# Front of a two-part kernel: x's maxima in four even pieces, the S4 parameters on GpSimd, and the attention masks loaded ahead of its first operands

## The chip, the cores and the metric

The kernel runs on one core of one Trainium2 chip. The metric is the device time of one launch in microseconds (us); lower is better. Engines are named as the profile names them: PE is TensorE (PEld its weight loads), DVE is VectorE, ACT is ScalarE, POOL is GpSimd, SP is SyncE, which here only issues DMAs. A line such as L743 is a line of the kernel before.

## The reference, cut to what matters

Two independent results stand side by side in the output.

```python
# A: sliding-window attention, x [2048, 576], 32 heads of 18, window 256
qkv = x @ wqkv                                # 576 -> 3 x 576
scores = q k^T * 18**-0.5, masked to 0 <= i-j < 256
a = (softmax(scores) v) @ wo
# B: S4 convolution, u [2048, 576], 128 states per channel
dt = exp(log_dt); dB = dt * B                 # per channel and state
K[d, l] = Re sum_n C * exp(dt*A*l) * dB       # 576 x 2048 filter taps
y = irfft(rfft(u) * rfft(K)) + u * Dskip      # causal convolution
out = concat([a, y], axis=-1)
```

Both are computed in float32 accuracy. For A, x and wqkv are scaled by a power of two, taken from their largest absolute value, and split into two float16 parts (high and low); three float16 products then stand for one float32 product. For B, the exponentials of a filter are built as products of small tables, summed over the states on PE, and the convolution is done by a two-stage transform.

## The kernel before

The program has three stages.

**The front** (`front`, about the first 62 us) loads wqkv in four column pieces (`wf`, in tile K), four row tiles of x (`raw`), the remaining rows of x as one flat array (`flat`, only for their maximum), the small parameters of B, and the S4 rates A. It finds the largest absolute values on DVE (`amax`, L170, into `amx`), reduces them over partitions on POOL (`pow2_max`, L155), and makes the scales: `sw` for wqkv (tile wr of the scalar steps), `sx` for x (tiles xg, xp, xr), `qsc` from both. Meanwhile PE runs `exact` (L217): the first six of the nine query/key products of the first 512 rows, in float32, 30 steps held in six PSUM banks until `qsc` is known; ACT runs the first exponentials (`exps`: tables mab and mg, L434), whose arguments PE makes (L417) from `al`, three bfloat16 parts of dt times A, written back by DMA (`level`). Each piece of wqkv is split by ACT (wh, L199) and DVE (wl, L201). The front is written in a manual order: on each engine the instructions stand as the code names them, except that work of the next stage may be moved up by the scheduler.

At its end the front splits the four row tiles of x (xh on ACT L228, xl and a second xh on DVE L229 and L230), takes exp of dt on ACT (L338) and forms eight products of 128x576 on DVE (L341 to L349): dt times B, and its complex product with C, giving the tiles wr and wi of 128x576 that the factors of B need.

**The middle** (about 62 to 396 us) merges three streams: `proj` (the split projections, L180, which write queries and keys through `qst` to DRAM), `tables` (factors on POOL L465 to L476, products m on POOL L487, tables Q on DVE L507 to L510, taps on PE L525 into `kp`), and `s1_u` (the first transform stage of u, L568). Here the scheduler sets the order on each engine. Held banks are released by `heads`, whose DVE half is `qst` (L367); the first value projections (L180) need such a bank.

**Attention and convolution** (from about 394 us). `att_setup` clears the operand tiles of three attention units; `attention_start` loads unit 0 from DRAM (`load_unit`, L722 and L723); `att_consts` (L701 to L708) clears `bias`, loads its two mask strips and the identity. `gmax` finds each row's largest score: DVE copies Q into qb (L734), PE makes scores r (L743), and DVE adds `bias` and reduces (jk, m, L750). `s1_k`, the transform of the taps K (L568 into pp), is merged with it, after DVE has added the skip term (L1089). The ring of scores has three banks, so PE can run only a few scores ahead of jk. From item 10 on the convolution is merged in (`conv_pools`, `conv`), whose first operands SP loads from L1118 and L595 on.

Each engine runs its instructions in order. [...]

Of the kernel before, what the change touches and what calls it, by code (L numbers as in the profile page):

```python
# [11 lines left out]
F32 = mybir.dt.float32  # L12
F16 = mybir.dt.float16
BF = mybir.dt.bfloat16
I32 = mybir.dt.int32
# [101 lines left out]
class Kernel:  # L117
# [115 lines left out]
    def front(self):  # L233


        nc, a, wp, sp, s4, tp = self.nc, self.a, self.p["wq"], self.p["const"], self.p["s4c"], self.p["prep"]
# [21 lines left out]
        cols = (0, 2304, 4608, 5760, 6912)  # L258
        for c in range(4):
            flat.append(tp.tile([128, 2304], F32, name="flat%d" % (c % 2))[:, :cols[c + 1] - cols[c]])  # L260
            nc.sync.dma_start(flat[c], a["xf"][:, cols[c]:cols[c + 1]])
# [39 lines left out]
        exact = self.exact(raw)  # L301
        for _ in range(15):
            next(exact)
        for c in range(4):
            self.amax(amx[:, c:c + 1], wf[c])
            if c < 3:
                level(c)
            if c < 2:
                for e in (2 * c, 2 * c + 1):
                    self.amax(amx[:, 4 + e:5 + e], raw[:, e])  # L310
        wm, wg = self.pow2_max(amx[:, 0:4], "w")
        pw, self.sw = self.pow2_of(wg, "w")
        steps = chain.from_iterable(zip(exps, exact))
        for _ in range(4):
            next(steps), next(steps)
        self.split_w(2, 0)
        self.amax(amx[:, 8:9], flat[0])
        self.split_w(2, 1)
        for _ in range(4):
            next(steps), next(steps)  # L320
        self.split_w(3, 0)
        self.amax(amx[:, 9:10], flat[1])
        for _ in range(4):
            next(steps), next(steps)
        for _ in chain(steps, exact):
            pass
        self.split_w(3, 1)
        for c in range(2, 4):
            self.amax(amx[:, 8 + c:9 + c], flat[c])
        xm, xg = self.pow2_max(amx[:, 4:12], "x")  # L330
# [9 lines left out]
        wi = self.wi = s4.tile([128, D], F32, name="wi")  # L340
        tt(par["B_re"], par["B_re"], dt, op=OP.mult)  # L341
# [345 lines left out]
    def att_setup(self):  # L687
        nc, a, ap = self.nc, self.a, self.p["att"]
        self.qb = ap.tile([128, 2, 32, 64], F16, name="qb")
        nc.gpsimd.memset(self.qb, 0.0)  # L690
        self.sets = []
        for b in range(3):
# [3 lines left out]
            for h in (32, 96):  # L696
                eng.memset(d["K"][h:h + 32].bitcast(I32), 0xF800F800 - (1 << 32))
# [3 lines left out]
    def att_consts(self):  # L701
# [5 lines left out]
        self.ident = ap.tile([128, 128], F32, name="ident")  # L707
        nc.sync.dma_start(self.ident, a["c_id"])  # L708
# [348 lines left out]
    def build(self):  # L1057
        nc, a = self.nc, self.a
        with ExitStack() as es:
# [36 lines left out]
            with self.tc.manual_schedule():  # L1096
# [3 lines left out]
                self.att_consts()  # L1100
# [12 lines left out]
                def conv_pools():  # L1113
# [4 lines left out]
                    nc.sync.dma_start(self.i2, a["c_i2"])  # L1118

# [38 lines left out]
```

## Time and profile before

| what | us |
|---|---|
| median of three timed runs (lowest, highest) | 979.88 (977.96, 983.45) |
| the profiled execution | 987.38 |
| its span, first to last instruction | 985.7 |
| PE busy in the span | 844.3 (86%) |
| DVE, ACT, POOL busy | 662.9, 566.0, 568.6 |

The profiled execution is 7.5 us above the median, at a mean granted PE clock of 0.965. PE is the busiest engine, but not in each stage: in slices of a fortieth of the span (24.6 us) its busy tenths begin 3758 and drop once more, to 5, just after 400 us. The questions are what PE waits for in the first 100 us, and what it waits for between 396 and 416 us.

### The profile page before, as it was taken

The numbers are of one execution on the slowest core, as the hardware profiler recorded it, in microseconds if no ns is written. First come the engines' busy times: TensorE is split into PE (matmuls) and PEld (weight loads), VectorE is DVE, ScalarE is ACT, GpSimd is POOL, SyncE is SP. The second block draws the span as 40 slices with busy tenths as digits, with TensorE's granted clock in tenths as the row PEclk, the third lists the DMA queues.
The fourth block names the chain that finished last, engine by engine and source line by source line (L and its number), as shares of the span: only waits on it lengthen the run. The fifth ranks groups of instructions, "written<-read, shape, count | busy, mean of one in ns | idle before, by whom it ended". The sixth has DMA issues, their size and how long they took to land.

```text
span 985.7 us, 26852 instructions
## 1 busy us (share of the span) xinstructions
PE 844.3 (86%) x10340; PEld 448.5 (46%) x10340; DVE 662.9 (67%) x1786; ACT 566.0 (57%) x917; POOL 568.6 (58%) x674
## 2 busy tenths in 40 slices
PE   3758897998999999589888888788888899999987
PEld 1235454564566557344433333333333444444445
DVE  5689678367565566456586878788777766667534
ACT  1556767565775765135665565565556555665770
POOL 3018878366677677502367775767675856635460
PEclk9879999899999999798999999999999999999999
DMA  9646354334443532443485665866655674387673
GB/s 314 174 142 177 101 139 115 96 90 113 127 106 78 134 94 77 155 163 124 149 167 144 168 164 145 196 140 171 141 146 138 155 192 106 106 225 199 197 202 129
DMA packets 137177, 145.32 MB, mean 147 GB/s; under 512 B 36553, under 2 KB 105337, under 8 KB 136665
## 3 DMA queue, kind: packets, MB, share of 16 engines
q1 hardware_dynamic: 131000, 131.45, 50.9%
q0 software_dynamic: 4592, 10.32, 3.9%
q10 hardware_dynamic: 1456, 1.84, 0.7%
q8 instruction: 81, 1.33, 0.6%
q14 instruction: 48, 0.39, 0.1%
HBM read 81.29 MB, written 61.01 MB: 144 GB/s over the span
## 4 chain that ended last, share of the span: by engine, by line
PE 45%; DVE 21%; issue 11%; ACT 8%; DMA 7%; POOL 5%; SPq 2%; DVEq 0%; ACTq 0%; POOLq 0%
PE pp L180 8%; PE po L807 6%; PE r L743 6%; PE r L1017 5%; PE kp L525 4%; PE r L609 3%; PE pp L568 3%; PE ST L784 3%; PE r L617 3%; DVE jk L750 3%; PE r L568 2%; PE x L417 2%; ACT P L786 2%; DVE qb L734 2%; DVE osb L866 2%
## 5 line engine op out<-in xcount | busy, mean ns | idle before, releaser
L750 DVE CUSTOM_DVE_ANT_0 jk<-r,bias 128x288 f32<-128x288 f32 (+7 forms) x512 | 199.8, 433 | 98.6 <-PE r L743 89.0
L795 POOL TENSOR_SCALAR_AFFINE_SELECT P<-P 128x512 f32<-128x512 f32 x240 | 166.4, 722 | 165.6 <-ACT P L786 163.2
L786 ACT ACTIVATE P<-ST,esc 128x1024 f32<-128x1024 f32 (+1 forms) x192 | 202.0, 1059 | 83.2 <-PE ST L784 82.9
L487 POOL TENSOR_TENSOR m<-A,tr 128x1024 f32<-128x1024 f32 x72 | 143.7, 2020 | 62.1 <-PE kp L525 62.1
L743 PE MATMUL r<-K,qb 128*64 128x288 f16 (+7 forms) x1024 | 130.9, 298 | 41.6 <-DVE qb L734 12.2
L743 PEld LDWEIGHTS <-qb 128*64 128x64 f16 x1024 | 58.2, 109 | 127.8 <-issue 74.4
L807 PE MATMUL po<-P,V 128*32 128x256 f32 (+2 forms) x1408 | 100.4, 397 | 12.7 <-ACT osb L815 4.4
L646 POOL TENSOR_TENSOR Y<-t,t 64x288 f32<-64x288 f32 x64 | 54.5, 852 | 67.6 <-DVE t L641 65.7
L525 PE MATMUL kp<-Q,m 128*32 128x64 f32 x4608 | 79.4, 221 | 9.5 <-issue 3.1
L525 PEld LDWEIGHTS kp<-Q,m 128*32 128x32 f32 x4608 | 68.8, 110 | 33.1 <-issue 21.4
L784 PE MATMUL ST<-Q,K 64*128 64x384 f16 (+2 forms) x704 | 73.2, 280 | 1.2 <-DMA Q<-mt 1.2
L465 POOL TENSOR_TENSOR tr<-tr,mab 128x768 f32<-128x768 f32 x18 | 33.4, 1858 | 44.0 <-ACT tr L434 44.0
L807 PEld LDWEIGHTS po<-P,V 128*32 128x32 f32 x1408 | 35.7, 109 | 47.1 <-issue 28.3
L647 POOL TENSOR_TENSOR Y<-t,t 64x288 f32<-64x288 f32 x64 | 52.4, 818 | 3.8
L428 DVE TENSOR_TENSOR k<-x,k 128x512 f32<-128x512 f32 (+1 forms) x54 | 33.9, 641 | 23.3 <-ACT k L427 22.8
L568 PE MATMUL pp<-ut,w 128*128 128x288 f32 x128 | 38.8, 429 | 10.6 <-DVE qst L367 6.1
L609 PE MATMUL r<-tx,w 128*64 128x288 f32 x256 | 42.0, 439 | 6.0 <-DVE m L750 3.8
L617 PE MATMUL r<-Y,i 128*128 128x288 f32 x128 | 42.8, 448 | 3.9 <-DVE t L642 1.2
L145 ACT ACTIVATE g<-pp 128x288 f32<-128x288 f32 x69 | 26.7, 412 | 32.5 <-PE pp L568 31.2
L609 PE MATMUL r<-tk,w 128*64 128x288 f32 x256 | 40.8, 424 | 4.8 <-DVE m L750 4.7
L434 ACT ACTIVATE mg<-x 128x512 f32<-128x512 f32 x72 | 39.9, 600 | 7.2 <-PE x L417 6.8
L367 DVE SCALAR_TENSOR_TENSOR qst<-pp,qst 128x512 f16<-128x512 f32 x30 | 20.6, 686 | 34.8 <-ACT qst L366 31.0
(192 smaller groups left out, 1713.8 us busy)
## 6 DMA issues: line engine op xcount, KB each, us to landing
qd<-qst SPq DMA_DIRECT2D x72, 128.0 KB
gx<-g SPq DMA_DIRECT2D x32, 288.0 KB
gk<-g SPq DMA_DIRECT2D x32, 288.0 KB
tx<-gx SPq DMA_DIRECT2D x32, 288.0 KB
tk<-gk SPq DMA_DIRECT2D x32, 288.0 KB
h<-ho SPq DMA_DIRECT2D x16, 576.0 KB
Q<-qd SPq DMA_DIRECT2D x32, 216.0 KB
raw<-in_x_dram SPq DMA_DIRECT2D x16, 320.0 KB
```

What stands on the lines that cost most here:

```text
L180: self.nc.tensor.matmul(ps, u, v, start=(i == 0), stop=(i == len(ops) - 1))
L487: self.nc.gpsimd.tensor_tensor(m, A[:, ch, a0:a0 + 8].unsqueeze(3).to_broadcast(sh), tr[:, ch, part, 0:8].unsqueeze(2).to_broadcast(sh), o ...
L525: nc.tensor.matmul(kp[32 * st:32 * st + 32, c % 2 * JJ2 + j, :], m[:, ch, a0:a0 + 32], Q[:, ch, term % 2, :], start=(term == 0), stop=(ter ...
L568: nc.tensor.matmul(ps, self.w1[:, part, :], src[:, o:o + k], start=True, stop=True)
L609: nc.tensor.matmul(ps[64 * par:64 * par + 64], w2[:, par, 64 * part:64 * part + 64], t[:, par, 2 * hs:2 * hs + 2, :], start=True, stop=True)
L617: nc.tensor.matmul(pair[par], i1[:, par, :], Y[par], start=True, stop=True)
L743: nc.tensor.matmul(ps[64 * b:64 * b + 64, :n], self.qb[:, b, t, :], d["K"][:, b, k0:k0 + n], start=True, stop=True, skip_group_check=True)
L750: nc.vector.tensor_tensor_reduce(out=jk[:, :n], in0=ps[:, :n], in1=self.bias[:, 288 - n:], scale=1.0, scalar=-3e38, op0=OP.add, op1=OP.max ...
L784: nc.tensor.matmul(ps[:, u, o:o + n], d["K"][h, jp, k0:k0 + 128], d["Q"][h, jp, q0:q0 + n], start=True, stop=True, skip_group_check=True)
L786: nc.scalar.activation(pt[:, 2 * jp:2 * jp + 2, lo:hi], ps[:, :, lo:hi], AF.Exp, scale=self.esc)
L795: nc.gpsimd.affine_select(v, v, pattern=[[0, 4], [sg, 128]], compare_op=OP.is_ge, fill=0.0, base=-1 if far else 0, channel_multiplier=-sg)
L807: nc.tensor.matmul(self.po[32 * j:32 * j + 32, t0 * 128:t1 * 128], V[:, kb * 76 + 19 * j:kb * 76 + 19 * j + 32], pt[:, j, o:o + (t1 - t0) ...
```

## The change

Six edits, all of them in placement and order, and a seventh move that follows from one of them; the arithmetic is the same.

1. `flat` has four equal pieces of 1728 columns in three buffers, before two of 2304 and two of 1152 in two buffers.
2. Of `exact`, 18 of 30 steps stand ahead of the first `exps` matmul, before 15; then one step follows every second `exps` matmul, and the rest comes last.
3. The maxima of all four `raw` tiles stand behind the first weight maximum. Both splits of the last two weight pieces start on ACT at once, and the flat maxima stand between their DVE halves.
4. The eight parameter products are POOL's.
5. `att_consts` is called at the start of `att_setup`, ahead of unit 0's loads; the identity is loaded with the convolution's constants.
6. The K tiles of the attention are cleared whole, by one instruction in place of two for 32 partitions each.
7. With 5, the scheduler places the addition of the skip term ahead of the first qb copy.

```diff
-        cols = (0, 2304, 4608, 5760, 6912)
+        cols = (0, 1728, 3456, 5184, 6912)
         for c in range(4):
-            flat.append(tp.tile([128, 2304], F32, name="flat%d" % (c % 2))[:, :cols[c + 1] - cols[c]])
+            flat.append(tp.tile([128, 1728], F32, name="flat%d" % (c % 3)))
             nc.sync.dma_start(flat[c], a["xf"][:, cols[c]:cols[c + 1]])
...
-        for _ in range(15):
+        for _ in range(18):
             next(exact)
         for c in range(4):
             self.amax(amx[:, c:c + 1], wf[c])
             if c < 3:
                 level(c)
-            if c < 2:
-                for e in (2 * c, 2 * c + 1):
+            if c == 0:
+                for e in range(4):
                     self.amax(amx[:, 4 + e:5 + e], raw[:, e])
         wm, wg = self.pow2_max(amx[:, 0:4], "w")
         pw, self.sw = self.pow2_of(wg, "w")
-        steps = chain.from_iterable(zip(exps, exact))
-        for _ in range(4):
-            next(steps), next(steps)
         self.split_w(2, 0)
+        self.split_w(3, 0)
         self.amax(amx[:, 8:9], flat[0])
         self.split_w(2, 1)
-        for _ in range(4):
-            next(steps), next(steps)
-        self.split_w(3, 0)
         self.amax(amx[:, 9:10], flat[1])
-        for _ in range(4):
-            next(steps), next(steps)
-        for _ in chain(steps, exact):
-            pass
         self.split_w(3, 1)
         for c in range(2, 4):
             self.amax(amx[:, 8 + c:9 + c], flat[c])
+        for n, _ in enumerate(exps):
+            if n % 2:
+                next(exact)
+        for _ in exact:
+            pass
         xm, xg = self.pow2_max(amx[:, 4:12], "x")
...
+        tt = nc.gpsimd.tensor_tensor
         tt(par["B_re"], par["B_re"], dt, op=OP.mult)
...
     def att_setup(self):
         nc, a, ap = self.nc, self.a, self.p["att"]
+        self.att_consts()
...
-            for h in (32, 96):
-                eng.memset(d["K"][h:h + 32].bitcast(I32), 0xF800F800 - (1 << 32))
+            eng.memset(d["K"].bitcast(I32), 0xF800F800 - (1 << 32))
...
-        self.ident = ap.tile([128, 128], F32, name="ident")
-        nc.sync.dma_start(self.ident, a["c_id"])
...
                 next(gm)
-                self.att_consts()
...
                     nc.sync.dma_start(self.i2, a["c_i2"])
+                    self.ident = self.p["fc"].tile([128, 128], F32, name="ident")
+                    nc.sync.dma_start(self.ident, a["c_id"])
```

How the change moves instructions is shown at three places. The first is DVE in the front, from the last step of the weights' scale (`wr 128x1`, L166) to the scale of x; `flat_...` are the pieces of x's rest, K is the weights' tile, 128x5x384 and 128x5x576 are the low halves of a weight piece.

```order
 L166 TENSOR_SCALAR wr<-wr 128x1
 L170 TENSOR_REDUCE amx<-flat_139 128x1
-L201 SCALAR_TENSOR_TENSOR wl<-K,wr,wh 128x5x384 x3
+L201 SCALAR_TENSOR_TENSOR wl<-K,wr,wh 128x5x384
 L170 TENSOR_REDUCE amx<-flat_141 128x1
 L201 SCALAR_TENSOR_TENSOR wl<-K,wr,wh 128x5x576
 L170 TENSOR_REDUCE amx<-flat_143 128x1
 L170 TENSOR_REDUCE amx<-flat_145 128x1
+L201 SCALAR_TENSOR_TENSOR wl<-K,wr,wh 128x5x384
 L154 TENSOR_REDUCE xm<-amx 128x1
+L201 SCALAR_TENSOR_TENSOR wl<-K,wr,wh 128x5x384
 L162 TENSOR_SCALAR xg<-xg 128x1
```

Two of the three low halves of 384 columns, which belong to the middle stage, now stand behind the flat maxima: one ahead of the maximum over them (xm), one between xm and the first step that reads POOL's reduction of it (xg).

The second place is DVE after the splits of the row tiles (L229, L230): the parameter products and the first two `qst`, which release held banks.

```order
 L230 SCALAR_TENSOR_TENSOR xh<-raw,xr,xh 64x128
-L341 TENSOR_TENSOR in_B_re<-in_B_re,dt 128x576
-L342 TENSOR_TENSOR in_B_im<-in_B_im,dt 128x576
-L344 TENSOR_TENSOR flat_143<-in_C_re,in_B_re 128x576
-L345 TENSOR_TENSOR flat_145<-in_C_im,in_B_im 128x576
-L367 SCALAR_TENSOR_TENSOR qst<-pp,qsc,qst 128x512
-L346 TENSOR_TENSOR wr<-flat_143,flat_145 128x576
-L347 TENSOR_TENSOR in_C_re<-in_C_re,in_B_im 128x576
-L348 TENSOR_TENSOR in_C_im<-in_C_im,in_B_re 128x576
-L367 SCALAR_TENSOR_TENSOR qst<-pp,qsc,qst 128x512
-L349 TENSOR_TENSOR wi<-in_C_re,in_C_im 128x576
```

The eight TENSOR_TENSOR rows are gone from here. On POOL they now stand behind the reduction xg and an instruction without operands (ISA), and ahead of four small DMA issues (dsk) and the first factor product (`tr<-tr,mab`).

The third place is DVE at the start of the attention, behind the last table of B. Before:

```order
L510 SCALAR_TENSOR_TENSOR Q<-sn,mg 128x16x32
L695 MEMSET Q_5864 128x1024
L697 MEMSET K_5865 32x1280 x2
L734 COPY qb<-Q_5864 54x64x32
L1089 TENSOR_TENSOR K<-K,dsk 128x144
L147 COPY g_5826<-pp 128x288
L734 COPY qb<-Q_5864 54x64x32
L704 MEMSET bias 128x288
```

and with the change (L693 stands for L695, L694 for L697, L1084 for L1089, L729 for L734, L701 for L704):

```order
L507 SCALAR_TENSOR_TENSOR Q<-sn,mg 128x16x32
L701 MEMSET bias 128x288
L693 MEMSET Q_5868 128x1024
L694 MEMSET K_5869 128x1280
L1084 TENSOR_TENSOR K<-K,dsk 128x144
L729 COPY qb<-Q_5868 54x64x32
L147 COPY g_5826<-pp 128x288
L729 COPY qb<-Q_5868 54x64x32
```

The clearing of bias is first, and the addition of the skip term (K<-K,dsk) has passed the first qb copy. On SP the two mask loads stand ahead of unit 0's four loads; before, they stood behind these and behind four stores of `gk`.

## The prediction

> **What bounds the kernel now.** I read the stages first (busy time by window), then the timelines of the engines in the two stages that the change touches, then the chain of waits there. Columns of the windows: length, busy time of PE, PEld, DVE, ACT, POOL (instructions), granted PE clock, DMA share, GB/s.
>
> ```profile
> 20.00:40.00 20.00, 15.46 (x34) 5.70 (x33) 14.37 (x15) 6.47 (x9) 4.29 (x9) 0.83 1.00 287
> 40.00:60.00 20.00, 13.73 (x37) 5.42 (x36) 16.65 (x19) 14.45 (x18) 2.30 (x5) 0.99 0.31 103
> 60.00:80.00 20.00, 14.89 (x91) 10.54 (x91) 16.98 (x31) 12.75 (x25) 7.00 (x8) 0.75 0.59 138
> 300.00:400.00 100.00, 91.65 (x2123) 60.51 (x2111) 64.27 (x98) 62.43 (x111) 76.27 (x57) 1.00 0.39 99
> 400.00:420.00 20.00, 12.71 (x49) 8.42 (x50) 6.38 (x27) 4.12 (x11) 8.22 (x11) 0.70 0.47 155
> ```
>
> The middle is PE's: 91.65 of 100 us. There an earlier start carries through, since behind about 110 us each engine's order is the same as before, up to the attention. The two ends are not PE's: from 20 to 40 us the DMAs are full, from 40 to 80 us DVE is busiest, from 400 to 420 us nobody is. PE's gaps there:
>
> ```profile
> 64.99 1.36 PE L180 MATMUL pp<-wh,xh 128*128 128x288 f16 x5 [9.83 <-DVE qst L367]
> ...
> 400.86 5.84 PE L568 MATMUL pp<-K,w 128*128 128x288 f32 x16 [4.91 <-DVE K L1089]
> ...
> 415.43 0.51 PE L743 MATMUL r<-K,qb 128*64 128x128 f16 x4 [6.23 <-DVE m L750]
> ...
> 417.67 4.11 PE L568 MATMUL pp<-K,w 128*128 128x288 f32 x8
> ...
> 424.46 2.21 PE L568 MATMUL pp<-K,w 128*128 128x288 f32 x8
> ```
>
> The first waits for the first qst, hence for x's scale; the second for the skip term; the third for jk. The same eight matmuls take 4.11 us after the third gap and 2.21 later: a gap also costs 1.90 of slow matmuls.
>
> **Part 1, x's scale (edits 1 to 3).** DVE between the two scales:
>
> ```profile
> 30.24 2.54 DVE L170 TENSOR_REDUCE amx<-flat 128x1 f32<-128x2304 f32 x1
> 37.09 2.22 DVE L201 SCALAR_TENSOR_TENSOR wl<-K,wr,wh 128x1920 f16<-128x1920 f32 x1 [4.30 <-ACT wh L199]
> 41.55 4.38 DVE L201 SCALAR_TENSOR_TENSOR wl<-K,wr,wh 128x1920 f16<-128x1920 f32 x2 [2.25 <-ACT wh L199]
> 45.85 2.55 DVE L170 TENSOR_REDUCE amx<-flat 128x1 f32<-128x2304 f32 x1
> 48.92 3.22 DVE L201 SCALAR_TENSOR_TENSOR wl<-K,wr,wh 128x2880 f16<-128x2880 f32 x1 [0.53 <-ACT wh L199]
> 52.06 2.60 DVE L170 TENSOR_REDUCE amx<-flat 128x1 f32<-128x1152 f32 x2
> 55.34 0.15 DVE L162 TENSOR_SCALAR xg<-xg 128x1 f32<-128x1 f32 x1 [0.48 <-POOL xg L155]
> ```
>
> The columns summed are the same, so DVE's work is: what can go is idle time, 4.30 + 2.25 + 0.53 = 7.1 us of waits for wh, and 0.48 for POOL's reduction, which a low half now covers. ACT made its first wh late because it stood behind an exponential:
>
> ```profile
> 34.78 0.49 ACT L434 ACTIVATE mab<-x 128x384 f32<-128x384 f32 x1 [8.16 <-DMA al<-part]
> 35.17 1.89 ACT L199 ACTIVATE wh<-K,wr 128x1920 f16<-128x1920 f32 x1
> ```
>
> Now two wh stand ahead of it; at 1.89 each and, for the wide one, half as much again (2.8), they end at 30.3 + 4.7 = 35.0, before the exponentials' data is there; DVE wants them at 32.2 (after one flat maximum of 1728 columns, 1.9) and 36. The other two follow by 41, and DVE wants them at 43. The fourth flat piece is the thin spot. Before, its issue waited for the second maximum (45.85 + 2.55 = 48.40):
>
> ```profile
> 48.42 0.35 SPq L261 DMA_DIRECT2D flat<-in_xf_dram  x1
> ```
>
> Now it waits for the first maximum, at 32. From 20 us on the DMAs still have the last weight piece (1.47 MB), flat (3.54), a row tile and parts of al and ps (about 1.0): 6.0 MB at 287 GB/s are 21 us, so it lands near 41, just when DVE gets to it. Price: **-7.6 us** for x's scale; bounds -4.6 (landing 3 us late) and -7.6 (no idle left). The reordered float32 products (edit 2) cost nothing: eight exponentials follow ACT's 41, at 0.65 each (0.49 for 384 columns in the row above, here 512), so the last ends near 46; seven steps of 0.9 (3.60 us for eight halves in the row below) end near 52.5, 2 us before PE can go on.
>
> ```profile
> 51.02 3.60 PE L217 MATMUL kp<-raw,K 128*128 128x512 f32 x8
> ```
>
> **Part 2, the parameters (edit 4).** On DVE the eight products stood between
>
> ```profile
> 61.51 0.76 DVE L341 TENSOR_TENSOR in_B_re<-in_B_re,dt 128x576 f32<-128x576 f32 x1
> ...
> 64.19 0.74 DVE L367 SCALAR_TENSOR_TENSOR qst<-pp,qsc,qst 128x512 f16<-128x512 f32 x1
> ```
>
> so the first qst comes 64.19 - 61.51 = 2.7 us earlier and, with all eight at a pitch of 0.67, what follows 5.4. With part 1 PE's values begin at 64.99 - 10.3 = 54.7, and DVE is 13.0 us ahead. But the factors need wr and wi, and POOL now has a queue ahead of them:
>
> ```profile
> 13.25 1.03 POOL L155 PARTITION_ALL_REDUCE zg<-zm  x1 [9.86 <-DVE amx L170]
> ...
> 55.47 1.95 POOL L355 DMA_DIRECT2D dsk<-in_dsk_dram  x4 [0.17 <-POOL xg L155]
> 72.75 1.82 POOL L465 TENSOR_TENSOR tr<-tr,mab 128x768 f32<-128x768 f32 x1 [15.32 <-ACT tr L434]
> 74.64 0.96 POOL L471 TENSOR_TENSOR t<-tr,wr 128x256 f32<-128x256 f32 x1
> 75.56 0.68 POOL L472 TENSOR_TENSOR t<-tr,wi 128x256 f32<-128x256 f32 x1
> ...
> 77.85 7.87 POOL L487 TENSOR_TENSOR m<-A,tr 128x1024 f32<-128x1024 f32 x4
> ...
> 94.20 1.82 POOL L465 TENSOR_TENSOR tr<-tr,mab 128x768 f32<-128x768 f32 x1 [3.11 <-ACT tr L434]
> ```
>
> One product of 128x576 is not in the trace. Between 0.68 (256 columns) and 1.82 (768) it lies at 1.4; bounds are 1.1 (7.87/4 x 576/1024) and 2.15 (0.96 x 576/256). I take 1.4, the nearest sizes: 11.2 us for eight. An ISA row without operands stands ahead of POOL's first reduction and of its first product, a change of code as I read it. Ahead of the first reduction POOL idled 9.86 us though zm was ready:
>
> ```profile
> 0.97 0.15 DVE L154 TENSOR_REDUCE zm<-halfpi 128x1 f32<-128x1 f32 x1
> ```
>
> Ahead of tr it lay within the 15.32 us idle. Now it comes behind the reduction of x's maximum, at about 46.0 (55.30 - 7.1 - 2.2, xm having one low half less ahead of it), so products can start between 46.0 + 9.9 = 55.9 and dt's exponential, whose end moves from 59.66 to 52.1:
>
> ```profile
> 58.99 0.67 ACT L338 ACTIVATE dt<-dt 128x576 f32<-128x576 f32 x1
> ```
>
> I take the middle, 54.0: the change of code should be shorter than all of that idle time. Then tr starts at 54.0 + 11.2 + 2.0 (dsk's issues) = 67.2, 5.5 earlier. The 3.11 us that POOL waited before the third tr (for DVE) close as well, since DVE is 13.0 ahead: -8.6. PE needs POOL's m for its taps, so POOL, not DVE, sets this stage: **-8.6 us**; bounds: 52.1 + 8.8 + 2.0 = 62.9, that is -9.9 - 3.1 = -13.0; and 55.9 + 17.2 + 2.0 = 75.1, that is +2.4 - 3.1 = -0.7. Part 1 is within this figure, not beside it.
>
> [...] The trace's 9.86 is only an upper limit.
>
> **Part 3, the masks (edits 5 to 7).** DVE and the chain of waits around 400 us:
>
> ```profile
> 399.03 1.56 DVE L734 COPY qb<-Q 54x2048 f16<-54x2048 f16 x1 [1.40 <-DMA Q<-qd]
> 400.52 0.28 DVE L1089 TENSOR_TENSOR K<-K,dsk 128x144 f32<-128x144 f32 x1
> ...
> 415.18 0.19 DVE L750 CUSTOM_DVE_ANT_0 jk<-r,bias 128x32 f32<-128x32 f32 x1 [7.90 <-DMA bias<-in_c_bias_dram]
> ```
>
> ```profile
> 396.22 1.04 ACT L533 ACTIVATE K<-kp 128x512 f32<-128x512 f32 x1 [3.84 <-PE kp L525]
> ```
>
> ```profile
> 408.19 6.82 DMA bias<-in_c_bias_dram
> ```
>
> The skip term needs only ACT's copy, done at 397.26, but stood behind a qb copy that waited for Q. Passed ahead, it ends at 397.6 and PE starts at 397.7: -3.2 of the 4.91. The mask loads now go ahead of unit 0's loads and land while Q does: the 6.23 us go too, and with them the slow matmuls behind that gap, 4.11 - 2.21 = 1.9. Sum **-11.3 us**; bounds -3.2 (another landing replaces the masks') and -12.7 (the sixteen matmuls at 400.86, 5.84 for 2 x 2.21, also run 1.4 faster). The Q and K loads are issued up to 1.0 later (two mask issues at 0.5, as the identity's below), hidden behind PE's sixteen matmuls, which end at 403.5, when qb's second half is done too; without that cover it costs 1.0. Clearing K whole is one instruction per tile, not two, of the same columns: no cost on DVE, some us saved on POOL off the path.
>
> The identity's load now stands on the chain ahead of the first convolution operands:
>
> ```profile
> 408.70 0.50 SPq L708 DMA_DIRECT2D ident<-in_c_id_dram  x1
> ```
>
> **+0.5 us**, bounds 0 and 1.
>
> **Sum**: -8.6 - 11.3 + 0.5 = -19.4 us on a profiled execution of 987.38, that is 968.0. That execution is 7.5 above the median; I take the same difference off 979.88: **960.5 us**. Least -0.7 - 3.2 + 1 = -2.9, 977; most -25.7, 954.
>
> **Rivals.**
>
> *POOL late* (15%): products at 2.15 after the longest change of code. Part 2 gives 0.7, the rest 10.8: 968.4. For it: two 256-column products took 0.96 and 0.68, so contention with DVE can show; against: larger ones stand near 1.9 ns per column. DVE's splits suffer from POOL too:
>
> ```profile
> 56.96 0.75 DVE L229 SCALAR_TENSOR_TENSOR xl<-raw,xr,xh 128x512 f16<-128x512 f32 x1 [0.51 <-ACT xh L228]
> ...
> 83.78 2.49 DVE L229 SCALAR_TENSOR_TENSOR xl<-raw,xr,xh 128x512 f16<-128x512 f32 x1
> ```
>
> 0.75 alone, 2.49 beside POOL's products; the new products bring that ahead of the first qst if POOL starts early (four such instructions, 1.4 each at most: 5.6 us, part 2 then -7.4, since DVE's 13.0 falls to that). [...]
>
> *Masks replaced* (12%): K's or Q's landing holds qb or r instead; part 3 gives 3.2 to 5: 967. For it: the four loads now stand behind the masks, and Q's landing held qb for 1.40 us before; against: PE has 5.8 us of matmuls meanwhile.
>
> *No carry-through* (9%): both gains vanish downstream, or the scheduler's new order up to about 110 us costs what the front saves and masks gain least: 977. Against it: PE's order is equal behind that.
>
> *Slower* (3%): POOL's queue ahead of the factors becomes the bound. It takes over 4.9 us net, so part 2 at +15.7: tr at 72.75 + 3.1 + 15.7 = 91.6, (91.6 - 55.9 - 2.0)/8 = 4.2 us per product. Beyond that: 985. No row is near.
>
> **How the numbers follow.** The forecast (parts 2 and 3 within some 4 us of their values) has 61%, with its own range 955 to 966. A change under 0.5% (4.9 us) can't be told from none here. Faster: 61 + 15 + 12 = 88%; same 9%; slower 3%. The range of 954 to 973 takes in the first two rivals and leaves the others out.
>
> **What would show it.** After the change: x's scale (xr) near 48.3 and no DVE wait over 1 us for wh before it; PE's first L180 near 55; the first tr on POOL at 63 to 70, right behind dsk; no wait of jk for bias; PE's first L568 on K 1.7 us behind the last taps. The prediction is wrong if tr starts after 72, if a wait for Q, K or bias over 3 us stands around 400, or if PE's shift at 390 us is under 5.

## The result and the profile after

The changed kernel takes 976.3 us (median of eight runs, 970.64 to 977.29) beside 983.4 us for the kernel before (median of eight, 977.96 to 984.97): ratio 0.9925, 95% interval 0.9898 to 0.9953, that is 7.1 us less. The forecast was 960.5 with a range of 954 to 973: the direction was right, the size was not, and the time lies 3 us outside the range. Timed once more on another chip (below), the changed kernel was 1.7 us faster by the medians, ratio 0.9969 (0.9936 to 1.0002), an interval that includes no gain. The first trace of the kernel before, from which the forecast was made, is of an execution at 987.4 us that was slow as a whole; two later traces of the same kernel are of 984.0 and 973.4 us, and the two of the changed kernel of 973.6 and 977.4.

Windows of the kernel after, with the columns of the prediction:

```profile
20.00:40.00 20.00, 17.97 (x45) 6.67 (x44) 18.59 (x16) 13.25 (x15) 4.27 (x9) 0.91 1.03 339
40.00:60.00 20.00, 15.36 (x66) 8.09 (x65) 17.72 (x28) 10.90 (x19) 8.59 (x6) 0.91 0.33 76
60.00:80.00 20.00, 16.13 (x97) 10.78 (x94) 17.09 (x20) 12.74 (x27) 19.64 (x18) 0.91 0.57 150
80.00:100.00 20.00, 12.93 (x381) 8.16 (x382) 15.54 (x22) 8.89 (x16) 17.35 (x17) 0.74 0.40 107
100.00:120.00 20.00, 16.07 (x212) 8.99 (x212) 11.79 (x19) 14.98 (x28) 13.53 (x11) 0.83 0.43 107
...
400.00:420.00 20.00, 15.26 (x79) 8.99 (x78) 13.46 (x46) 5.36 (x14) 6.07 (x9) 0.91 0.70 225
```

From 20 to 40 us DVE now works 18.59 of 20 us (14.37 before), and from 400 to 420 us PE works 15.26 (12.71 before). The new hole is between them: from 80 to 100 us PE works only 12.93 us, at a granted clock of 0.74. PE's gaps there and at the start of the attention:

```profile
53.52 1.30 PE L180 MATMUL pp<-wh,xh 128*128 128x288 f16 x5 [4.64 <-DVE qst L364]
...
85.49 1.33 PE L565 MATMUL pp<-ut,w 128*128 128x288 f32 x2 [7.33 <-ACT g L145]
...
112.82 1.14 PE L522 MATMUL kp<-Q,m 128*32 128x64 f32 x18 [3.48 <-DVE Q L505]
...
398.34 3.18 PE L565 MATMUL pp<-K,w 128*128 128x288 f32 x12 [1.48 <-DVE K L1084]
404.71 1.86 PE L565 MATMUL pp<-K,w 128*128 128x288 f32 x4 [3.19 <-DVE g L147]
...
406.76 3.10 PE L565 MATMUL pp<-K,w 128*128 128x288 f32 x8
```

PE begins its values 11.5 us earlier than before (64.99), and then waits 7.33 us for a g copy on ACT and 3.48 us for a table on DVE, neither of which it did before. Of the two old gaps at 400 us, the one for the skip term is down from 4.91 to 1.48 us and the one for jk is gone, but PE now waits 3.19 us for a g copy on DVE, and eight matmuls behind that take 3.10 us, not 2.21.

The front itself went as forecast. From DVE and POOL:

```profile
46.86 0.16 DVE L165 RECIPROCAL xr<-xp 128x1 f32<-128x1 f32 x1
```

```profile
53.57 1.39 POOL L338 TENSOR_TENSOR in_B_re<-in_B_re,dt 128x576 f32<-128x576 f32 x1 [7.13 <-ACT xh L228]
54.94 1.84 POOL L339 TENSOR_TENSOR in_B_im<-in_B_im,dt 128x576 f32<-128x576 f32 x1
...
67.56 2.21 POOL L462 TENSOR_TENSOR tr<-tr,mab 128x768 f32<-128x768 f32 x1
...
85.90 1.81 POOL L462 TENSOR_TENSOR tr<-tr,mab 128x768 f32<-128x768 f32 x1
```

Where the gain goes is seen by following stations (start times in us, from the timelines; the copies are ACT's K<-kp, one for each block of filter taps; jk is counted from 0). The first three columns are of the first traces; the last is the mean of both traces of the changed kernel less the mean of all three of the kernel before:

| station | before | after | difference | of the means |
|---|---|---|---|---|
| scale of x (xr) | 55.72 | 46.86 | -8.9 | -7.2 |
| first tr on POOL | 72.75 | 67.56 | -5.2 | -3.7 |
| third tr on POOL | 94.20 | 85.90 | -8.3 | -6.8 |
| first copy of taps | 101.49 | 97.00 | -4.5 | -3.0 |
| second copy | 116.75 | 111.05 | -5.7 | -4.0 |
| third copy | 125.60 | 126.02 | +0.4 | +1.6 |
| last (18th) copy | 396.22 | 396.91 | +0.7 | +2.8 |
| first jk | 415.18 | 407.11 | -8.1 | -3.0 |
| jk number 32 | 441.41 | 433.79 | -7.6 | -1.6 |

All of the front's gain is given back by the third copy, most of it between the second and the third, and the 270 us behind it keep the loss. What gain there is arises between the last copy and the attention. Its size can't be read from one pair of traces: 8 to 9 us by the first pair, 4 to 6 by the means.

### The profile page after: what moved, and what is told of

Its sections match the earlier page's. It is cut to its first block, busy times and chain, and to the rows that moved or that the text cites. A ratio compares the mean times of both kernels' runs of the same rounds, so it can differ in the third digit from the quotient of the medians.

```text
span 971.9 us, 26837 instructions
## 1 busy us (share of the span) xinstructions
PE 839.5 (86%) x10340; PEld 447.2 (46%) x10340; DVE 666.5 (69%) x1777; ACT 565.2 (58%) x917; POOL 579.2 (60%) x680
## 3 DMA queue, kind: packets, MB, share of 16 engines
q10 hardware_dynamic: 1456, 1.84, 0.6%
## 4 chain that ended last, share of the span: by engine, by line
PE 50%; DVE 17%; issue 11%; ACT 7%; DMA 6%; POOL 6%; SPq 2%; DVEq 0%; ACTq 0%; POOLq 0%
PE pp L180 9%; PE po L802 6%; PE r L738 6%; PE r L1012 5%; PE kp L522 4%; PE pp L565 4%; PE r L606 3%; PE r L614 3%; PE ST L779 3%; DVE jk L745 3%; PE x L414 2%; DVE qb L729 2%; PE r L565 2%; DMA raw<-in_x_dram 2%; DMA K<-in_wqkv_dram 2%
## 5 line engine op out<-in xcount | busy, mean ns | idle before, releaser
L565 PE MATMUL pp<-ut,w 128*128 128x288 f32 x128 | 41.2, 453 | 15.6 <-ACT g L145 11.0
L426 DVE TENSOR_SCALAR ab<-k 128x512 int32<-128x512 int32 (+1 forms) x54 | 50.5, 946 | 1.7 <-POOL wr L343 1.3
L180 PE MATMUL pp<-xh,wh 128*128 128x512 f16 x150 | 43.1, 406 | 0.0
```

Source lines behind the costliest of these rows:

```text
L180: self.nc.tensor.matmul(ps, u, v, start=(i == 0), stop=(i == len(ops) - 1))
L565: nc.tensor.matmul(ps, self.w1[:, part, :], src[:, o:o + k], start=True, stop=True)
```

## The experiments

Two questions were open: what took the front's gain between 78 and 126 us, and what the mask edits are really worth. The kernel before was timed again beside each group.

### What took the front's gain

**Masks alone and front alone.** The first kernel is the one before with edits 5 to 7 and nothing else; the second is the changed one without them.

> The kernel before with edits 5 to 7 alone (masks first, whole K tiles, skip term ahead of the first qb copy). Theory 1 (the front's gain is given back between 78 and 126 us, the masks carry the whole measured gain): 7 to 9 us below the kernel before, ratio near 0.992, that is the changed kernel's own time within 2 us; the last copy of the taps (K<-kp) within 1 us of 396.2 us, the first jk 8 us earlier, near 407. Rival (the front's gain survives in part, the masks are worth less): 3 to 5 us below, ratio near 0.996.

> The changed kernel without edits 5 to 7, so the front's four edits alone. Theory 1: no gain, ratio 0.998 to 1.002; x's scale near 47 and the first qst near 52.7 as in the changed kernel, but the third copy of the taps (K<-kp) at 126 and the last at 396 to 397. Rival (front's gain survives in part): 3 to 7 us below the kernel before, ratio near 0.995. By the prediction's part 2 it would be 8.6 us below, ratio 0.991.

The masks alone: 977.5 us against 980.7, ratio 0.9975 (0.9941 to 1.0009). The front alone: 980.4, ratio 1.0021 (0.9980 to 1.0062), with xr at 46.60, the first qst at 52.48, the third copy of the taps at 126.15 and the last at 395.62. The masks gave 3.2 us by the medians and 2.4 by the ratio, near the rival, with an interval that includes no gain; the 7 to 9 us of theory 1 did not come, though the first jk, at 405.87, was as early as it said. The front's edits bring nothing as they are, as theory 1 said, and the reason lies in the front's own consequences, not in the masks.

**POOL or the order?** POOL was the first suspect, since the trace names it. ACT's timeline before, and then after, round the third tr:

```profile
90.07 0.67 ACT L366 ACTIVATE qst<-kp,qsc 128x512 f16<-128x512 f32 x1
90.64 0.40 ACT L386 ACTIVATE vst<-pp 128x288 f32<-128x288 f32 x1
90.93 0.71 ACT L145 ACTIVATE g<-pp 128x288 f32<-128x288 f32 x2
91.88 0.41 ACT L145 ACTIVATE g<-pp 128x288 f32<-128x288 f32 x1 [0.24 <-PE pp L568]
92.69 0.52 ACT L434 ACTIVATE tr<-k 128x384 f32<-128x384 f32 x1 [0.40 <-DVE k L428]
```

```profile
83.05 0.52 ACT L431 ACTIVATE tr<-k 128x384 f32<-128x384 f32 x1 [5.11 <-POOL m L484]
...
84.46 0.68 ACT L363 ACTIVATE qst<-kp,qsc 128x512 f16<-128x512 f32 x1
85.03 1.01 ACT L145 ACTIVATE g<-pp 128x288 f32<-128x288 f32 x3
```

```profile
72.96 5.89 POOL L484 TENSOR_TENSOR m<-A,tr 128x1024 f32<-128x1024 f32 x3
78.81 2.25 POOL L462 TENSOR_TENSOR tr<-tr,mab 128x768 f32<-128x768 f32 x1
81.02 2.00 POOL L484 TENSOR_TENSOR m<-A,tr 128x1024 f32<-128x1024 f32 x1
```

Before, the g copies stand ahead of the third tr. After, the scheduler has put the third tr ahead of them; tr has two buffers, and the first is free when POOL's fourth m has read it, at 83.0. That m in turn now stands behind the second tr. ACT waits 5.11 us with the g copies behind it, and PE waits for g.

The first test puts the eight products back on DVE, which also brings back the order of before on POOL; the second leaves every order as it is and takes 2 us off POOL.

```diff
-        tt = nc.gpsimd.tensor_tensor
```

> The changed kernel with the eight parameter products back on DVE (edit 4 undone, edits 1 to 3 and 5 to 7 kept); the order on POOL is then that of before, with four m ahead of the second tr. Theory 1 (POOL's change of code, eight products and the late m hold ACT at the third tr's buffer, and PE starves behind it): the first tr on POOL at 64 to 66, no wait of PE over 4 us between 75 and 100 us, the third copy of the taps at 118 to 121, and the time 4 to 7 us below the changed kernel, 12 to 15 below the kernel before, ratio near 0.987. Rival theory 2 (the stage's start is paced by something else, such as DVE or the DMAs or the clock behind a gap): the third copy of the taps at 125 to 127 and the time within 2 us of the changed kernel's.

```diff
+            nc.sync.dma_start(self.dsk[32 * e:32 * e + 1], a["dsk"][:, 144 * e:144 * e + 144])
...
-            nc.gpsimd.dma_start(self.dsk[32 * e:32 * e + 1], a["dsk"][:, 144 * e:144 * e + 144])
```

> The changed kernel with the four dsk loads issued on SP at the front's start instead of on POOL behind the products; every other row on every engine keeps its place. It takes 2 us off POOL ahead of its first tr. Theory 1 (POOL is what is late): the first tr at 65.5 instead of 67.6, PE's wait of 7.33 us at 85 down to 5 to 6, and the time 1 to 2 us below the changed kernel's. Theory 2 (something else paces): the first tr earlier, but the same wait of PE and the same time within 1 us.

With the products on DVE: 969.1 us, ratio 0.9898 (0.9849 to 0.9947), a little less gain than theory 1 said, 5 us below the dsk variant on the same chip; first tr 64.83, third copy 118.46. With dsk on SP: 974.4 us, ratio 0.9945 (0.9911 to 0.9979); the first tr did come at 65.75, but PE's wait was 7.44 us, not 5 to 6, only earlier, and of the 2 us that the third copy showed (123.93) nothing was left at the fourth (150.59, against 150.74). So 2 us less on POOL bought nothing at the station, as theory 2 said; undoing the edit, which moves both POOL's load and the order, bought some 7 us there.

These two effects are parted by the number of products that POOL takes. With the first three on DVE and the last five on POOL the scheduler chooses PE's and (from the third tr on) ACT's order of before; with the first six on POOL it chooses ACT's of the changed kernel.

```diff
-        tt = nc.gpsimd.tensor_tensor
-        tt(par["B_re"], par["B_re"], dt, op=OP.mult)
+        tt = nc.vector.tensor_tensor
+        tg = nc.gpsimd.tensor_tensor
+        tt(par["B_re"], par["B_re"], dt, op=OP.mult)
...
-        tt(y2, par["C_im"], par["B_im"], op=OP.mult)
+        tg(y2, par["C_im"], par["B_im"], op=OP.mult)
...
```

> The changed kernel with the first three parameter products on DVE and the last five still on POOL. With this split the scheduler's order on PE, and on ACT from the third factor table on, is that of products all on DVE (and so of before): g copies ahead of the third tr, four m ahead of the second tr. If the order is what gives the front's gain back: no PE wait over 4 us between 75 and 100 us though POOL still carries five products, the third copy of the taps at 118 to 121 as with all products on DVE, and the time 4 to 7 us below the changed kernel's. If POOL's products themselves are what is late: the third copy at 123 to 126 and the time within 2 us of the changed kernel's.

> The changed kernel with the last two parameter products on DVE, so six on POOL, one more than in the run with five. The scheduler's order on ACT is that of the changed kernel (the third tr ahead of the g copies), only POOL has four m ahead of its second tr; POOL is 2.8 us earlier, and the fourth m ends near 78 to 79 us rather than 83.0. If ACT's place of the third tr behind POOL's fourth m is what costs: PE's wait for g falls from 7.3 us to 2 to 4, the third copy of the taps lies between (120 to 124 us), and the time 2 to 4 us below the changed kernel's. If the order as a whole, not that wait, costs the gain: the third copy at 124 to 126 and the time within 1.5 us of the changed kernel's.

Five on POOL: 969.7 us against 977.1 for the changed kernel on the same chip, ratio to before 0.9898 (0.9845 to 0.9951). Six on POOL, on another chip: 979.1 us, ratio 0.9992 (0.9956 to 1.0028). One product more, with other products on DVE, and another order, and the gain is gone. The third copy of the taps, with five and then with six:

```profile
116.75 1.05 ACT L531 ACTIVATE K<-kp 128x512 f32<-128x512 f32 x1
```

```profile
128.58 1.04 ACT L531 ACTIVATE K<-kp 128x512 f32<-128x512 f32 x1 [2.56 <-PE kp L523]
```

And PE with six on POOL:

```profile
67.72 4.21 PE L566 MATMUL pp<-ut,w 128*128 128x288 f32 x8 [2.79 <-ACT vst L384]
...
86.22 1.12 PE L566 MATMUL pp<-ut,w 128*128 128x288 f32 x2 [2.56 <-ACT g L145]
...
114.58 1.15 PE L523 MATMUL kp<-Q,m 128*32 128x64 f32 x20 [3.48 <-DVE Q L506]
```

The wait for g shrank from 7.33 to 2.56 us, as expected for an earlier POOL, and yet the third copy came later than in the changed kernel, and later than either theory had said. So the one wait that the trace shows largest is not what costs: another stands at 67.7 us, and the 3.48 us at 114 us, where taps stand next in PE's queue, is the same to the hundredth in this kernel, the changed one and the dsk variant.

That the loss goes with the order is shown: five kernels with this order on PE and ACT have their third copy at 123.9 to 128.6, five with that of before and an early front at 116.7 to 119.9. That POOL is late does not explain it: the dsk variant starts its third tr at 83.95, earlier than any of the five that keep the gain (85.3 to 86.3), and its first two copies (94.36 and 108.68) are level with those of the kernel with all products on DVE (94.58 and 109.61). No run changes the order and nothing else, since each new order came with another split of the products.

Where most is lost can be read from the copies. From the second to the third, 8.8 to 8.9 us pass in all eleven traces with the order of before, with the old front or the new, and 13.9 to 15.8 in all six with the changed order. These six, and no other, show the wait of 3.48 us for Q. PE before, and then behind that wait in the changed kernel:

```profile
112.71 1.72 PE L568 MATMUL pp<-ut,w 128*128 128x288 f32 x6
114.36 0.54 PE L525 MATMUL kp<-Q,m 128*32 128x64 f32 x24
...
116.32 0.75 PE L568 MATMUL pp<-ut,w 128*128 128x288 f32 x2 [0.77 <-ACT g L145]
```

```profile
113.89 4.21 PE L565 MATMUL pp<-ut,w 128*128 128x288 f32 x8
```

Before, six of these eight transform matmuls stand ahead of the second copy (116.75). After, all eight stand behind it, and behind 18 taps whose Q is not ready. Part of the longer stretch is thus work that moved into it: from the first to the third copy, 23.8 to 24.5 us became 28.5 to 30.1. Whether the eight could have run during the wait no run shows, so which row of the order costs most stays open, beyond that it is not the wait for g alone.

The gap at 112 us costs twice. PE's granted clock in the changed kernel behind it:

```profile
108.00:112.00 4.00, 1.34 (x55) 0.74 (x43) 3.97 (x5) 3.99 (x7) 3.35 (x2) 0.96 0.42 87
112.00:116.00 4.00, 3.11 (x23) 2.15 (x24) 3.94 (x8) 2.49 (x6) 3.92 (x5) 0.50 0.66 171
116.00:120.00 4.00, 4.00 (x14) 2.10 (x13) 1.86 (x4) 1.23 (x3) 1.30 (x3) 0.69 0.42 139
120.00:124.00 4.00, 4.00 (x166) 2.79 (x168) 2.27 (x5) 3.44 (x6) 2.04 (x1) 1.00 0.31 76
```

Read in steps of 1 us, the clock was 0.50 from 112 to 118 us and 0.77 in the next. Half the clock for about 6 us: by an estimate from the two windows, this gap of 3.48 us cost some 3 us more (4.0 x 0.50 + 4.0 x 0.31). With five on POOL the 40 us from 80 on ran at full clock, though PE waited 3.06 us at 82, and PE worked 34.05 us of them, 29.00 after the change:

```profile
80.00:100.00 20.00, 15.03 (x421) 9.67 (x422) 14.68 (x25) 13.11 (x24) 16.48 (x15) 1.00 0.48 125
100.00:120.00 20.00, 19.02 (x440) 11.75 (x438) 15.76 (x28) 16.68 (x31) 15.84 (x13) 1.00 0.53 130
```

So in the changed kernel 3.48 us of idleness were followed by some 6 us at a granted clock of 0.50; with five on POOL it is 1.00 in both windows.

**The front with its order kept, alone.** Last, the five-on-POOL front without the mask edits, to price part 2 by itself, and beside it the same front with them.

> The front's four edits with five products on POOL, hence with the scheduler's order of before on ACT, PE and POOL behind 110 us, and without edits 5 to 7. If the prediction's part 2 had the size right and only the order took it away: 7 to 9 us below the kernel before, ratio 0.991 to 0.993, the third copy of the taps (K<-kp) at 116 to 118, the last at 387 to 390. If the front's gain needs the masks' edits too, or goes elsewhere in the middle: the last copy at 393 to 396 and under 4 us of gain.

> Front with five products on POOL and the masks' edits, once more, beside the run without these edits. The difference of the two times is the price of the masks' edits with a front that keeps its gain: 3 to 5 us by the two timings of the masks alone, 7 to 9 by the traces' jk number 32, 11.3 by the prediction's part 3.

Without the mask edits: 972.7 us against 980.3, ratio 0.9923 (0.9892 to 0.9954), so 7.5 us of gain (4.5 to 10.6), third copy 118.84, last 392.46. With them: 966.5, ratio 0.9863 (0.9825 to 0.9900). The one trace, of an execution at 980.6 us, has the third copy 1 us later than expected and the last between the two cases, so the size of the gain rests on the times. With the order kept, the front is worth about what part 2 said (8.6), but not by part 2's means: all eight products on DVE gave the same ratio (0.9898) as five on POOL (0.9898, and 0.9863 here). So the gain comes with the earlier scale of x, and no gain from moving products to POOL is shown. The masks' edits are worth 6.2 us by these two medians, 6.8 by the means, give or take some 3.

### What the masks are worth

**How steady is the price?** The masks' landing was taken from one execution. Here are more traces of the kernel before, and one more timing of the masks alone.

> The kernel before once more, for a second trace. Its first profiled execution is 6 to 7 us above the mean of its other executions. If that excess lies in the transition and the attention: the last copy of the taps (K<-kp) within 1 us of 396.2, the wait for the first jk about 4.9 us rather than 6.23 and the eight matmuls behind it near 3 us rather than 4.11 (as in the run with the front's edits alone, whose transition is the same code), jk number 32 near 438.6 rather than 441.4, and the whole near 981. Then the masks' price in the trace was overstated by 2 to 3 us. If not: the same stations as in the first trace within 1 us.

> The kernel before, a third trace. From the last copy of the taps to jk number 32: 45.2 and 41.7 us in the two traces so far, 43.0 in the run with the front's edits alone. If the wait for the masks varies with the DMA queues, it lies between 41 and 46, and the wait of PE for jk between 3 and 6.5 us.

> The kernel before with edits 5 to 7 alone, once more. By the traces (jk number 32 at 36.1 us behind the last copy of the taps, against 43.0 to 45.2 without the edits) it should be 7 to 9 us below the kernel before; by its first timing it is 3 us below. If the timing was right and the trace's gain is given back in the attention: 2 to 4 us below again, and 542 to 544 us from jk number 32 to the end. If the first timing was low by chance: 6 to 9 us below, and 538 to 541 us from there to the end.

The second and third trace of the kernel before (issue-to-landing rows of the chain of waits, then DVE's first jk), one after the other:

```profile
406.24 3.96 DMA bias<-in_c_bias_dram
```

```profile
403.32 1.75 DMA bias<-in_c_bias_dram
```

```profile
410.37 0.19 DVE L750 CUSTOM_DVE_ANT_0 jk<-r,bias 128x32 f32<-128x32 f32 x1 [5.04 <-DMA bias<-in_c_bias_dram]
```

```profile
405.24 0.19 DVE L750 CUSTOM_DVE_ANT_0 jk<-r,bias 128x32 f32<-128x32 f32 x1 [2.83 <-DMA bias<-in_c_bias_dram]
```

The second trace agrees with its expectation only in that the transition is shorter: jk number 32 at 436.7, not at 438.6, PE's wait shorter than said, the eight matmuls behind it no faster, and the attention as long as in the first. The third lies outside what was expected: 37.1 us, not 41 to 46, and a wait of 1.16, not 3 to 6.5. The landing that the forecast took at 6.82 us was 3.96 and 1.75 us in other executions of the same kernel, and PE's wait behind it, 6.23 in the forecast, was 3.31 and 1.16 (4.89 and 5.13 in the two front-only kernels, whose code is the same there). The mean of the five is 4.1 us, and the forecast's is the largest. The matmuls behind, 4.11 us in the forecast, took 4.21, 2.21, 2.94 and 3.16.

So the whole transition varies. From the last copy of the taps to jk number 32, in us:

| kernels | traces | mean |
|---|---|---|
| without edits 5 to 7 | 45.2, 41.7, 37.1 (before), 43.0, 43.7 (fronts alone) | 42.1 |
| with them, as in the change | 36.9, 37.0 (changed), 36.1, 33.5 (masks alone), 35.1, 36.8, 37.0, 33.5, 37.9 (others) | 36.0 |

The means differ by 6.1 us, as the medians of the last pair do (6.2). The masks alone, timed twice, gave 3.2 and 3.6 us by the medians, 2.4 and 4.6 by the ratios (the second 976.1 against 979.7, ratio 0.9953, 0.9919 to 0.9987), with intervals that reach to 5.8 and 7.9. From jk number 32 to the end the second trace of the masks alone took 543.2 us. By the medians both numbers are those expected if the gain were given back in the attention; but kernels without the edits take 541.4 to 545.5 us there, so that it is given back is not shown. The times of the kernel before scatter over some 16 us, so the last 2 to 3 us of this price stay open.

**What took the place of the old waits.** In the changed kernel DVE's first qb copy, 0.69 us when alone, takes 4.88, and DVE's g copy, for which PE waits, stands behind it. DVE, then POOL:

```profile
399.42 4.88 DVE L729 COPY qb<-Q 54x2048 f16<-54x2048 f16 x1 [1.13 <-DMA Q<-qd]
404.23 0.43 DVE L147 COPY g<-pp 128x288 f32<-128x288 f32 x1
404.69 0.69 DVE L729 COPY qb<-Q 54x2048 f16<-54x2048 f16 x1
```

```profile
397.95 1.79 POOL L693 MEMSET Q<- 128x2048 f16 x1
399.69 1.16 POOL L694 MEMSET K<- 128x1280 int32 x1
400.80 1.79 POOL L693 MEMSET Q<- 128x2048 f16 x1
402.55 1.16 POOL L694 MEMSET K<- 128x1280 int32 x1
```

POOL's last clear ends at 403.71 and the copy 0.59 us later. The next run undoes edit 6; its diff is the two lines of edit 6 turned round.

> The changed kernel with edit 6 undone: each K tile cleared by two instructions for 32 partitions, as before. In the changed kernel the first qb copy on DVE takes 4.88 us while POOL clears whole tiles, against 1.56 before, and PE waits 3.19 us for the g copy behind it. If the whole K clears on POOL are what hold the copy: the copy at 1.5 to 2, no PE wait over 1 us for g, the first jk 3 to 4 us earlier (near 403.5) and the time 3 to 4 us below the changed kernel's. Rival (the clears of the Q tiles, or any clear on POOL, hold it just as long): copy at 4 us or more, first jk near 407, time within 1 us.

```profile
401.12 0.74 DVE L730 COPY qb<-Q 54x2048 f16<-54x2048 f16 x1 [0.35 <-DMA Q<-qd]
```

The copy took 0.74 us and the wait for g was gone, as the first theory said, but PE waited 1.71 us for the second qb copy instead, the first jk came 8.7 us behind the last copy of the taps, 9.6 in the changed kernel on the same chip, and the time was the same (977.2 and 977.1). DVE clears its own K in two instructions too, so the skip term was 1.0 us later, and the second qb copy now waited 1.29 us for Q's second load. The rival's reason, that any clear holds the copy as long, is refuted; its time, within 1 us, is what came.

In two of nine traces with whole clears the copy also got through early, in the second trace of the masks alone (DVE, then POOL):

```profile
397.93 1.46 DVE L732 COPY qb<-Q 54x2048 f16<-54x2048 f16 x1 [1.53 <-DMA Q<-qd]
```

```profile
397.69 1.16 POOL L697 MEMSET K<- 128x1280 int32 x1
398.80 2.34 POOL L696 MEMSET Q<- 128x2048 f16 x1
```

There it ended 0.54 us behind the first K clear, and the Q clear was longer by 0.54 us (2.34, 1.80 for the Q clear ahead). By these times the copy waited for one clear, and the next clear for the copy; in the changed kernel the copy (4.88 us) waited for all that were queued. What decides between the two no run shows.

**The clears out of the way.**

```diff
-        nc.gpsimd.memset(self.qb, 0.0)
...
+        self.clear(0, nc.vector)
+        self.clear(1, nc.gpsimd)
+        self.clear(2, nc.gpsimd)
...
+                nc.vector.memset(self.qb, 0.0)
```

> Products on DVE as in the earlier run, and in addition the clear of qb moved from POOL to DVE, so that POOL's clears of units 1 and 2 begin 3.5 us earlier and are over when the first qb copy starts. If POOL's clears are what hold the qb copy: both copies at 0.7 us each, no PE wait over 1 us for g, K's addition of the skip term up to 1.5 us later, the first jk 2 to 3 us earlier relative to the last copy of the taps (K<-kp), and the time 2 to 3 us below that of the run with products on DVE, near 967, 14 below the kernel before. If they are not: copies at 4 us still, and the time the same or 1 us above.

> The best of the runs so far put together: three products on DVE, five on POOL (the order of before), and the clears of units 1 and 2 ahead on POOL, that of qb on DVE. If the two gains add: the last copy of the taps near 387 us, the first jk near 397, and the time 11 to 14 us below the kernel before, ratio 0.986 to 0.989. If the clears bring nothing where the float32 matmuls run at half clock behind the wait for the skip term: the same time as with five products on POOL alone within 1.5 us, ratio 0.989 to 0.991.

With all products on DVE the copies took 1.05 and 0.69 us, about as expected, but the first jk was 10.6 us behind the last copy of the taps (9.4 with the products on DVE alone): the skip term stood behind qb's clear, PE waited 3.14 us for it and then ran its sixteen matmuls in 6.99 us, and the second Q load landed 2.95 us after DVE wanted it. 969.0 us, ratio 0.9869 (0.9828 to 0.9911); with five products on POOL 967.6, ratio 0.9877 (0.9836 to 0.9919), with the last copy (390.30) and the first jk (399.46) some 3 us later than expected. That ratio is one expected for gains that add, but so is the 0.9863 of five on POOL with the clears left as they were. Beside 969.1, 969.7 and 966.5 without the edit, on other chips in part, no difference is shown. The best version is a simpler one, with the clears left as they were: five products on POOL, at 969.7 and 966.5 us, or all eight on DVE, at 969.1, which these timings do not tell apart.

**The changed kernel again.**

> The changed kernel once more, beside the others on the same chip: 6 to 8 us below the kernel before, ratio 0.992 to 0.994. Its trace against the first one shows how much one execution differs from another: the third copy of the taps within 1 us of 126.0, the PE wait near 85 us at 7.3, the first jk within 2 us of 407.1, and all differences over 2 us behind 430 us, in the attention.

It was 977.1 us against 978.9, 4 to 6 us less gain than expected (3 to 5 by the ratio), with the third copy at 125.61 and the first jk at 407.35, both as in the first trace. PE had its wait for g again (8.17 us), and from jk number 32 on took 540.9 us, 538.1 in the first trace. Over all traces that last stretch is 538.0 to 545.5 us with no order by kernel that these runs show.

## Why the prediction was right or wrong

- **Part 1, x's scale at 48.3.** Right in kind, and 46.86 came. DVE waits for no wh at all before it, and its flat maxima waited for no load. The station itself scatters: 53.0 to 55.7 in five traces with the old front, 46.5 to 47.5 with the new. The trace that the forecast used is the latest of the five; by the means (54.25 and 46.89) the shift is -7.4, almost the -7.6 said.
- **Part 2, POOL's products.** The steps up to the third tr were right: products from 53.57 (54.0 said), 1.39 to 1.84 us each (1.4), first tr at 67.56 (67.2), third tr at -8.3 (-8.6; -6.8 by the means), the 3.11 us gap closed. That 54.0, the middle of a range of 3.8 us, was met has some luck in it: dt's exponential ended at 50.80, not 52.1, and POOL stayed idle for 7.13 us behind its reduction (7.0 to 7.4 in six such traces), where 8.0 had been allowed (reading it as a change of code was the author's inference from POOL's idle times). The step behind them, "so POOL, not DVE, sets this stage", failed: 2 us less on POOL brought nothing, and with all eight products on DVE the gain was there.
- **"There an earlier start carries through, since behind about 110 us each engine's order is the same as before."** This step failed, and it took part 2's 8.6 us with it: the shift of the last copy was +0.7 (+2.8 by the means). The equal order begins where the gain is already gone: between 60 and 126 us ACT, PE and DVE have another order, and no term was set for what it costs; 5 to 7 us more from the second copy of the taps to the third are what the traces show. With the order kept, the gain did carry through to the end (7.5 us by the times), so the reason given holds where its condition does.
- **Rival No carry-through (9%).** It named what came: that the scheduler's new order up to about 110 us costs what the front saves. That the argument against it was "PE's order is equal behind that" was the same oversight. Its time, 977, took the masks at their least, 3.2 us; the two timings of the masks alone gave 3.2 and 3.6, the traces and the last pair 6. That 976.3 and 977.1 were measured is in part luck.
- **Rival POOL late (15%).** Products were not late. POOL's reduction of xm took 2.24 us beside a low half on DVE (0.35 before), and DVE operations were slower beside the products (1.40 us for a split's low half, 0.75 alone), but the third tr came at 85.90 all the same.
- **Part 3, the masks at -11.3.** Mis-sized: 3 to 6 us. The skip term passed as said (PE's wait 1.48, from 4.91). The 6.23 us was the largest of five executions and the 1.9 the second largest; their means are 4.1 and 1.1, the latter from 1.90, 2.00, 0.00, 0.73 and 0.95. And "no cost on DVE, some us saved on POOL off the path" missed that POOL's clears now meet the qb copy: 3.19 us of PE's wait in place of the old one.
- **Rival Masks replaced (12%).** Its time for part 3, 3.2 to 5, is near what the two timings of the masks alone gave; its mechanism, a load landing late, was not what held qb in the changed kernel (DVE waited 1.13 us for Q there). Where the clears were out of the way it did show: the second half of Q came 1.29 to 2.95 us late.
- **The sum.** -19.4 became about 0 for the front (-2 to +6 by the run of the front alone) and -3 to -6 for the masks. The signs that were named worked: all held except the shift at 390 us, which was named as the one that would show the forecast wrong if under 5, and was +0.7. That the profiled execution of before was 7.5 us above its median was taken off the sum, but not off the terms, and part of it lay in the very wait that part 3 removed.

## What to carry to other kernels

Where a scheduler sets the order, an edit upstream changes it downstream. A gain counts only from the point where the order is again the same; the stretch ahead of that point needs its own price, and a small move between engines can be enough to keep the old order or lose it (five products on POOL and six, each beside the kernel before, differed by 9 us). The longest wait of a stage need not be what costs: here it shrank from 7.33 to 2.56 us and nothing came of it. The wait for a DMA's landing varied from run to run, from 6.82 to 1.75 us for the same code; a term like that, and the stations it is read from, need more than one trace.

## What was not expected of the hardware

- The f16 copy of 54x2048 on DVE took 0.69 us alone and 4.1 to 4.9 us beside POOL's clears of whole 128-partition tiles, in seven of nine traces until POOL's last clear had ended; beside clears of 32 partitions the first of the two took 0.69 to 1.60.
- POOL's reduction of xm over partitions took 2.24 us beside a low half on DVE (`wl<-K,wr,wh`, 2.21 us; 12 traces), 0.35 us without one (5 traces).
- The kernel before varies over 16 us from run to run (971.9 to 988.0, without its few slowest); the masks' landing, 1.75 to 6.82 us, and the eight matmuls behind it, 2.21 to 4.21 us, are two of the parts that were seen to vary.
